# Two chunks' state products interleaved over the tile array, and a new order of the first up stage

## The chip, the cores and the metric

The kernel runs on one core of one Trainium2 chip. The metric is the device time of one execution in microseconds (us). Kernels are compared by the median of several runs.

## The reference, cut to what matters

```python
gamma = 1.0 - 2.0 ** (-5.0 - np.arange(H))            # H = 8 heads
for t in range(S):                                     # retention: q, k, v are (B=4, H=8, S=768, D=64)
    state = gamma * state + einsum('bhd,bhe->bhde', k[:, :, t], v[:, :, t])
    y[:, :, t] = einsum('bhd,bhde->bhe', q[:, :, t], state) / sqrt(D)
x = y.transpose(0, 2, 1, 3).reshape(B * S, H * D)      # 3072 tokens x 512
g = x @ w_gate                                         # 512 x 1536
out = (g * sigmoid(g) * (x @ w_val)) @ w_out           # 1536 x 512
```

The weights come as float64 words, and the kernel turns them into float32 itself.

## The kernel before

**Segments.** The tokens are worked in four segments of 768: three chunks of 128 positions of two batches each. Segment 0 has the chunks c = 0, 6, 1, 7, 2, 8 (batch 0 and batch 1 in turn; `cs[0]` to `cs[5]`). For each segment the attention makes `x`, an up stage makes the hidden values of 12 column blocks (filters f = 0 to 11), and a down stage multiplies by `w_out`. The attention of segment 1 is woven into the down stage of segment 0, and so on. The change is in segment 0, whose attention, weight conversion and up stage run together in the first 105 us or so.

**Attention of a chunk.** Transposed keys and queries lie with the two heads of a pair on partitions 0 to 63 and 64 to 127 (`half[0]`, `half[1]`); each product of a head uses the rows of its own half.
- `scores` (L633 for TensorE, PE): eight products with 64 rows into two banks, one bank per head of a pair; VectorE (DVE) multiplies each bank with the decay mask (L639). The masks are the first three pieces of the table `tab`, which is loaded in pieces A0, A1, A2, A4 (6 KB) and A3 (query decays).
- `rows_of` (L694) transposes the keys of the first two chunks on PE, so that their rows need not be loaded. `scale_k` (L654 on DVE or GpSimd, POOL; L661 on ScalarE, ACT) and `scale_q` (L648) put the decays on keys and queries.
- `state` (L715): keys times values, 64 rows of output per head. Of a batch's first chunk ACT copies it (L718), later DVE adds it (L720) to the old state that `decay` (L701, four ACT instructions) has scaled.
- `mix_old` (L730): old state times queries, eight products of 64 rows by 64 columns of the array, heads in turn, so two 64x64 tiles of the array are in use; one chunk after the other.
- `mix` (L744): values times masked scores, into the same bank; then the result is split in three parts into `xa` (ACT L1000, DVE L1007 and L401).

**Weights.** Raw halves (gate, value) of a filter are loaded (L513), and converted: ACT L534 and L537, DVE L547, ACT L540, DVE L555. Filters 0 and 1 are converted half by half, gate first. The converted block is split in three parts as a matmul operand: ACT L991, DVE L994, POOL L997.

**Up stage of segment 0.** Filters 0 and 1 go in pieces of one chunk pair (`plain_part`, L937, 12 matmuls of 256 columns each, one piece for gate and one for value); filters 2 to 11 go whole (`plain`, L919). Each piece needs all three parts of its operands, the third last.

**What sets the order.** `PLAN` is a list of steps written out by hand, and every engine's queue has its instructions in that order. `s0` is `scores(cs[0])`, `m` mix, `o` mix_old, `t` state, `r` rows_of, `g` decay, `K`, `k`, `E`, `Q`, `q` the scalings, `x` a split, `l3:1` a load of chunk `cs[3]`, `A` a table piece; `U`, `V` raw weight loads, `a`, `b`, `S`, `c`, `C` the conversion, `n` the three parts of the two halves, `p`, `v`, `u`, `y` the pieces, `G`, `W`, `i`, `j` the whole filters. Loads are issued by the sync engine (SP) in one queue (the first two query chunks by ACT), with at most eight under way: each load waits for the one eight before it. The segments after that, and the down stages, are in the same list.

**Last segment.** In its down stage, the blocks of `w_out` come by one load each (768 KB), for the first three filters by two (L1147).

Of the kernel before, what the change touches and what calls it, by code (L numbers as in the profile page):

```python
# [55 lines left out]
    C1:0 l5:2 p0:1 n1:1 u0:0 u0:1 T0:0 q5 v0:1 a2 l4:2 b2 y0:1 o5 y0:0 o4 n1:3 S2 n1:2 m5 T0:1 n1:4  # L56
    c2 m4 n1:5 x5:2 p1:0 l5:3 x5:1 p1:1 u1:0 C2 v1:0 U3:1 T0:2 x4:2 T1:0 U12:0 a3 v1:1 y1:0 x4:1
    T1:1 L b3 p0:2 a12 c12 n2:0 S3 u1:1 T1:2 b12 u0:2 U4:3 c3 Z0 n2:1 v0:2 Z1 n2:3 S12 y1:1 a4 n2:2
    p1:2 v1:2 C3 u1:2 n2:4 G2:0 y0:2 C12 G2:1 n3:0 U13:1 y1:2 n3:1 n2:5 b4 T2:0 n3:2 S4 U5:2 n3:3
    c13 T2:1 W2:0 Z12 W2:1 h0 c4 i2:1 n3:4 i2:0 G3:0 n3:5 T3:0 C4 T2:2 T3:1 U6:3 j2:0 a5 G3:1 T3:2  # L60
    j2:1 Z2 n4:0 U7:0 W3:0 i3:0 n4:1 b5 n4:2 n4:3 S5 n4:4 W3:1 i3:1 n4:5 c5 G4:0 C5 n5:0 a6 b6 a13
    l4:3 T4:0 j3:0 G4:1 n5:1 j3:1 Z3 T4:1 n5:3 i4:0 n5:2 T4:2 S6 W4:0 b13 c6 i4:1 n5:4 a7 S13 C6
    W4:1 n6:0 T5:0 U8:2 Z4 b7 U14:3 n5:5 n6:1 G5:0 j4:1 S7 C13 j4:0 G5:1 n6:2 a8 n6:3 P2 n6:4 i5:1
    c14 W5:1 i5:0 Z13 c7 j5:1 T6:0 n6:5 W5:0 a14 U9:1 U15:0 C7 T5:1 G6:0 T6:1 n7:0 T5:2 G6:1 n7:3
    n7:1 T6:2 i6:0 b8 j5:0 Z5 S8 n7:4 W6:1 b14 g4 n7:2 G7:0 i6:1 W6:0 P0 c8 S14 C8 Z6 C14 h2 a9 b9
    G7:1 j6:1 n7:5 S9 n8:0 c15 n8:3 j6:0 k5 c9 W7:1 Z14 T7:0 n8:1 C9 n8:4 U10:2 a15 n8:2 i7:1 U11:1
    W7:0 T7:1 j7:1 n8:5 i7:0 T8:0 T7:2 b15 Z7 S15 a10 n9:0 G8:0 G8:1 W8:1 i8:0 n9:3 b10 j7:0 T8:1
    n9:1 n9:2 U16:3 S10 a11 n9:4 G9:0 k4 i8:1 t4 C15 c10 C10 n9:5 W8:0 g5 n10:0 T8:2 T9:0 b11 c16
    n10:1 G9:1 Z15 j8:0 j8:1 n10:2 a16 n10:3 t5 U17:2 b16 W9:0 i9:1 T9:1 0/h0.0 T9:2 S11 Z8 W9:1 S16
    G10:1 n10:4 i9:0 C16 c11 C11 n10:5 n11:0 j9:0 Z9 G10:0 n11:3 Z16 i10:1 j9:1 a17 i10:0 W10:1 P1  # L70
    n11:4 T11:0 T11:1 1/was0.0 T11:2 n11:1 W10:0 Z11 c17 n11:2 n11:5 b17 0/h0.1 0/W0 G11:1 0/h1.0
    G11:0 j10:0 0/d0.0 h1 0/h0.2 1/sc0 j10:1 i11:0 0/h1.1 0/W1 S17 0/d1.0 i11:1 0/d0.1 1/l3 C17
    T10:0 1/dec0.0 W11:0 0/d1.1 0/d0.2 W11:1 0/h2.0 j11:0 0/D0.2 j11:1 1/k0.0 1/l4 1/dec0.1 1/q0.0
    0/D0.1 1/q0.1 0/D0.4 1/k0.1 1/l5 0/D0.0 0/h2.1 0/d1.2 0/h1.2 0/h4.0 0/W2 0/Z0 1/A0 1/y0.06
    1/new0.0 0/h4.1 1/y0.01 0/D0.5 0/D0.3 0/d2.0 1/B0 0/D1.1 0/h3.0 1/y0.03 0/D1.5 1/y0.04 0/Z1
    1/y0.02 1/y0.07 1/y0.05 T10:1 1/was0.1 1/y0.15 1/y0.00 1/y0.14 0/d2.1 0/D1.4 1/y0.12 0/d2.2
    0/D1.2 1/y0.13 0/W3 Z17 0/D1.3 0/Z2 0/d3.0 0/D1.0 0/h2.2 0/h3.1 1/C0 0/W4 T10:2 0/h3.2 0/d3.1
    0/h4.2 Z10 1/y0.16 1/l7 1/y0.17 1/new0.1 1/sum0.0 0/D2.3 0/D2.1 1/y0.10 0/h5.0 1/begin 1/sum0.1
    0/d3.2 0/h5.1 1/y0.11 0/D2.5 1/sc1 0/D2.0 0/d4.0 1/was1.0 0/D2.4 0/d4.1 0/D3.4 1/l6 1/dec1.1
    0/h5.2 1/dec1.0 0/D2.2 1/x0.2.0 0/D3.1 1/q1.1 0/d4.2 0/W5 0/D3.5 1/x0.1.0 0/h6.0 1/k1.0 0/Z3  # L80
    1/sum0.3 1/k1.1 1/sum0.2 1/x0.2.1 0/D4.5 0/D3.2 0/D3.3 0/D3.0 1/q1.0 0/Z4 0/h6.1 0/D4.0 0/D4.4
    1/x0.1.2 1/x0.1.1 1/A1 1/x0.0.0 0/d5.0 1/x0.2.2 1/y1.00 0/h6.2 1/y1.06 1/x0.0.2 1/new1.0 0/D4.2
    0/d5.1 0/d5.2 0/D4.3 0/D4.1 1/y1.07 1/y1.01 0/W6 0/h7.0 1/B1 1/x0.0.1 1/y1.04 1/y1.12 0/h7.1
    1/l9 0/d6.0 0/D5.4 0/h8.0 0/d6.1 1/y1.02 0/D5.3 0/D5.2 0/W7 0/h8.1 1/y1.05 0/d6.2 1/l8 1/l11
    0/Z5 1/y1.03 1/was1.1 0/D5.5 1/C1 0/d7.0 1/y1.16 0/d7.1 0/D6.5 0/D5.0 1/y1.17 1/y1.15 1/new1.1
    0/h7.2 1/y1.14 1/y1.11 0/D5.1 1/y1.13 1/x1.2.0 0/D6.3 0/d7.2 0/D6.4 0/Z6 1/y1.10 0/D7.3 0/h9.0
    1/sc2 0/h8.2 1/x1.2.2 0/D6.2 1/q2.1 1/k2.1 0/D7.5 0/W8 1/sum1.0 0/D6.1 1/sum1.2 1/k2.0 0/D6.0
    0/D7.1 1/x1.1.0 0/h10.0 0/h9.1 0/d8.0 0/D7.2 1/dec2.0 1/l10 1/sum1.1 1/dec2.1 0/W9 1/x1.1.1
    0/D7.0 0/d8.1 1/x1.2.1 0/Z7 1/sum1.3 1/was2.0 1/q2.0 1/x1.0.0 1/x1.1.2 0/d9.0 0/D7.4 0/d8.2
    0/h11.0 1/A2 1/new2.0 0/D8.0 1/x1.0.1 0/h10.1 0/D8.3 0/D8.2 0/d9.1 1/L0 0/D8.1 1/y2.00 0/D8.4  # L90
    1/B2 0/W10 0/d9.2 1/y2.07 1/y2.05 0/d10.0 0/D8.5 0/h9.2 1/y2.02 0/h11.1 0/D9.3 1/y2.03 0/h10.2
    1/y2.01 0/D9.5 0/Z8 1/y2.04 1/y2.06 1/w0.0.0 0/D9.4 0/d10.1 0/h11.2 1/C2 1/y2.16 1/y2.14 0/W11
# [12 lines left out]
    1/p3.4 1/u3.4 1/u2.2 1/u2.8 1/p3.5 1/u3.1 1/u3.5 1/L6 1/w5.1.0 1/p3.6 1/w4.0.2 1/u2.9 1/w4.1.2
    1/u3.6 1/w5.0.0 1/w4.2.1 1/p4.1 1/w5.0.1 1/p4.0 0/e5 2/begin 1/w5.2.0 1/w5.0.2 1/u3.8 1/p4.3
    1/u4.0 1/w5.1.1 1/u4.4 1/u3.9 1/w5.2.1 1/p4.2 1/u4.3 1/L7 1/u3.2 1/w5.1.2 1/p4.5 1/p5.0 1/u4.1
    1/p4.4 1/u4.5 1/w6.1.0 1/p5.1 1/u5.0 1/w4.2.2 1/w6.0.0 1/w6.1.1 1/p5.2 1/u5.1 1/u4.6 0/e4
    1/w6.1.2 1/u2.7 1/w6.0.1 1/w6.2.0 1/w5.2.2 1/u5.3 1/p4.6 1/p5.3 1/p5.4 1/u5.4 1/u4.8 1/p5.5
    1/u5.5 1/L8 1/w7.2.0 1/p5.6 1/u4.9 1/w6.0.2 1/u4.2 1/w7.1.0 1/w8.2.0 1/p6.1 1/u5.6 1/w7.0.0  # L110
    1/u4.7 1/w7.2.1 1/p6.0 1/u3.7 1/w7.1.1 1/w7.0.1 1/u6.0 1/w8.2.1 1/u5.2 1/u6.1 1/L10 1/p6.3
    1/w7.0.2 1/u6.4 1/u5.8 1/p6.2 1/p6.5 1/u5.9 1/u6.3 1/u6.2 1/p6.4 1/w7.2.2 1/u5.7 1/w7.1.2
    1/w8.1.0 1/w6.2.1 1/p7.0 1/u6.6 1/w6.2.2 1/p7.3 1/p7.1 1/u6.5 1/p6.6 1/u7.0 1/L9 1/w8.0.0
    1/w8.1.1 1/u7.4 1/p7.2 1/p7.5 1/w8.0.1 1/u6.8 1/w9.2.0 1/u6.9 1/u7.3 1/u7.1 1/w9.2.1 1/u7.6
    1/w8.0.2 1/p7.4 1/p8.0 1/u8.0 1/w8.1.2 1/p8.1 1/u7.5 1/w9.1.0 1/p8.3 1/w9.1.1 1/w9.0.0 1/p8.2
    1/u8.4 1/u8.3 1/p7.6 1/u7.2 1/p8.5 1/L11 1/u7.8 1/w9.1.2 1/w9.0.1 1/w8.2.2 1/p8.4 1/u8.6 1/u6.7
# [254 lines left out]
def tile_retnet_swiglu(  # L371
# [249 lines left out]
    def pairs(t):  # L621
        return t.rearrange("p (n t) -> p n t", n=NP)
# [717 lines left out]
```

## Time and profile before

| | us |
|---|---|
| median of 3 runs (lowest, highest) | 643.47 (642.88, 643.62) |
| the profiled execution | 642.54 |
| its span, first to last instruction | 640.5 |
| PE busy | 632.9 (99%) |
| DVE, ACT, POOL busy | 484.1, 394.3, 261.1 |
| first scores on PE start at | 5.78 |
| last mix of segment 0 ends, up pieces of filter 1 begin | 34.22 |
| whole filters (L919) begin | 46.14 |

PE's work is almost the whole span. In the table above, the last three rows are stages of segment 0 read from PE's timeline. In the profile's lines, `64*64` ahead of a shape is the tile of the PE array (rows by columns), a float32 matmul leaves two records (`x16` is eight matmuls), and `[0.60 <-DMA ...]` is idle time just before a row and what ended it. Times of PE's rows overlap a little, since matmuls are pipelined: the distance between two starts says more than a row's own length.

### The profile page before, as it was taken

Reading aid. Unit: us, or ns where it says so; the run is one execution under the profiler, and the core shown is the slowest. Engines: PE = TensorE matmul, PEld = TensorE weight load, DVE = VectorE, ACT = ScalarE, POOL = GpSimd, SP = SyncE. Lnnn points to the kernel's source line nnn. Section 1 sums busy time; section 2 is a strip of 40 time slices with the busy share of each in tenths; the row PEclk is TensorE's granted clock in tenths of the full one; section 3 lists DMA queues with packets and bytes.
Section 4 is the critical chain, followed back from the end, with each engine's and each line's share of the span. In section 5 each row is a group of like instructions: output and inputs, shape, how many; then the busy total and the mean of one; then the engine's idle time right before and its main releaser. Section 6 shows DMA issues by size and latency. Waiting matters only on the chain.

```text
span 640.5 us, 14132 instructions
## 1 busy us (share of the span) xinstructions
PE 632.9 (99%) x5587; PEld 580.4 (91%) x5587; DVE 484.1 (76%) x715; ACT 394.3 (62%) x868; POOL 261.1 (41%) x172
## 2 busy tenths in 40 slices
PE   7999999999999999999999999999999999999997
PEld 6899999987779999997778999998777999999886
DVE  4998787899898887665797869575789866768361
ACT  4787797777865565566766555564785555654221
POOL 1534445544425866630003665550101666663000
PEclk9999999999999999999999999999999999999999
DMA  9899998798787445258765640457776444304564
GB/s 320 291 332 326 376 329 269 268 326 305 266 285 278 168 148 173 75 179 260 247 239 214 211 152 15 175 196 246 226 258 248 154 164 173 116 1 151 194 214 148
DMA packets 50626, 139.60 MB, mean 218 GB/s; under 512 B 5120, under 2 KB 18176, under 8 KB 50560
## 3 DMA queue, kind: packets, MB, share of 16 engines
q1 hardware_dynamic: 49984, 137.92, 62.6%
q8 instruction: 44, 0.72, 0.5%
q10 hardware_dynamic: 576, 0.79, 0.3%
q14 instruction: 22, 0.18, 0.1%
HBM read 108.80 MB, written 29.88 MB: 217 GB/s over the span
## 4 chain that ended last, share of the span: by engine, by line
PE 97%; DMA 3%; SPq 0%; DVE 0%; ACT 0%; issue 0%
PE bank L1088 41%; PE bank L1157 32%; PE bank L919 13%; PE bank L789 6%; PE bank L937 3%; DMA hT<-in_v_n_dram 2%; PE bank L744 1%; DMA hT<-in_q_t_dram 1%; PE bank L730 0%; PE bank L715 0%; PE bank L633 0%; DVE chunk_x L1178 0%; SPq L513 0%; ACT chunk_x L1180 0%; SPq L466 0%
## 5 line engine op out<-in xcount | busy, mean ns | idle before, releaser
L1157 PE MATMUL bank<-oitem,gitem 128*128 128x512 f32 x867 | 208.2, 394 | 0.0
L1157 PEld LDWEIGHTS bank<-oitem,gitem 128*128 128x128 f32 x867 | 159.6, 188 | 34.5 <-DVE tmp L812 0.4
L997 POOL TENSOR_TENSOR gitem<-gitem 128x768 fp32r<-128x768 f32 x71 | 138.7, 1963 | 117.9 <-DVE gitem L994 99.0
L1088 PE MATMUL bank<-xa,gitem 128*128 128x384 f32 x864 | 160.5, 334 | 0.0
L1088 PEld LDWEIGHTS bank<-xa,gitem 128*128 128x128 f32 x864 | 150.8, 188 | 0.2
L997 POOL TENSOR_TENSOR oitem<-oitem 128x256 fp32r<-128x256 f32 (+1 forms) x60 | 64.1, 1074 | 56.8 <-DVE oitem L994 48.3
L1088 PE MATMUL bank<-xb,gitem 128*128 128x384 f32 x432 | 84.5, 334 | 0.0
L919 PE MATMUL bank<-xa,oitem 128*128 128x384 f32 x480 | 84.3, 335 | 0.0
L919 PEld LDWEIGHTS bank<-xa,oitem 128*128 128x128 f32 x480 | 83.0, 188 | 0.4 <-ACT tmp L444 0.2
L994 DVE SCALAR_TENSOR_TENSOR gitem<-gitem,loads 128x768 fp32r<-128x768 f32 x72 | 75.1, 1057 | 9.1 <-ACT gitem L991 7.5
L1088 PEld LDWEIGHTS bank<-xb,gitem 128*128 128x128 f32 x432 | 75.9, 188 | 0.4
L991 ACT ACTIVATE gitem<-loads 128x768 fp32r<-128x768 f32 x72 | 59.6, 843 | 26.0 <-PE bank L1088 16.8
L994 DVE SCALAR_TENSOR_TENSOR gitem<-gitem,hT 128x768 fp32r<-128x768 f32 x48 | 46.1, 965 | 24.4 <-ACT gitem L991 24.4
L991 ACT ACTIVATE gitem<-hT 128x768 fp32r<-128x768 f32 x48 | 40.2, 842 | 31.4 <-PE bank L1157 29.4
L1022 ACT COPY chunk_x<-bank 64x128 f32<-64x128 f32 x144 | 36.6, 260 | 32.6 <-PE bank L789 21.3
L401 DVE SCALAR_TENSOR_TENSOR gitem<-gitem 128x768 fp32r<-128x768 f32 x49 | 49.7, 1022 | 1.3 <-DVE gitem L994 0.5
L816 POOL TENSOR_TENSOR loads<-loads,tab 128x512 f32<-128x512 f32 x9 | 13.4, 1493 | 82.1 <-PE bank L789 44.6
L1088 PE MATMUL bank<-xb,oitem 128*128 128x384 f32 x216 | 43.4, 335 | 0.0
L1088 PEld LDWEIGHTS bank<-xb,oitem 128*128 128x128 f32 x216 | 37.9, 188 | 0.3
L994 DVE SCALAR_TENSOR_TENSOR oitem<-oitem,loads 128x256 fp32r<-128x256 f32 (+1 forms) x42 | 34.5, 824 | 2.1 <-ACT oitem L991 2.1
L1105 DVE TENSOR_TENSOR hT<-bank,tmp 128x384 f32<-128x384 f32 x36 | 20.0, 555 | 20.7 <-PE bank L1088 20.4
L1103 ACT COPY tmp<-bank 128x384 f32<-128x384 f32 x36 | 17.2, 478 | 28.3 <-PE bank L1088 19.3
(118 smaller groups left out, 789.8 us busy)
## 6 DMA issues: line engine op xcount, KB each, us to landing
loads<-wup SPq DMA_DIRECT2D x36, 896.0 KB, 4.7
oitem<-wdnt SPq DMA_DIRECT2D x33, 768.0 KB, 4.4
wdnt<-oitem SPq DMA_DIRECT2D x12, 768.0 KB, 5.5
wup<-first SPq DMA_DIRECT2D x9, 896.0 KB, 6.7
rawp<-in_w_gate_dram SPq DMA_DIRECT2D x12, 512.0 KB, 6.8
rawp<-in_w_val_dram SPq DMA_DIRECT2D x12, 512.0 KB, 6.2
rawp<-in_w_out_dram SPq DMA_DIRECT2D x12, 512.0 KB, 5.7
out_dram<-chunk_x SPq DMA_DIRECT2D x21, 256.0 KB, 2.1
```

What stands on the lines that cost most here:

```text
L401: stt(o, x, 1.0, y, op0=mul, op1=op)
L789: nc.tensor.matmul(o, a, b, start=start, stop=True, skip_group_check=True)
L919: nc.tensor.matmul(o, w[:, a, ts(b, P)], X0[:, a, i, NC - 1 - b], start=a == b == 0, stop=a == 2 and b == NC - 1, skip_group_check=True)
L937: nc.tensor.matmul(o, w[:, a, ts(b, P)], X0[:, a, :, NC - 1 - b, ts(j, P)], start=a == b == 0, stop=a == 2 and b == NC - 1, skip_group_che ...
L991: act(o[0], x, AF.Copy, scale=CUT / FAR)
L994: stt(o[1], f32(o[0]), -FAR, x, op0=mul, op1=add)
L997: op(o[2], f32(o[0]), f32(o[1]), op=add)
L1022: copy(cx[half[i], ds(2 * h, 2), c, half[z]], y.rearrange("p (b t) -> p b t", b=2))
L1088: nc.tensor.matmul(o, w[:, a, k], x[:, a, KH - 1 - k], start=start and a == k == 0, stop=a == 2 and k == KH - 1, skip_group_check=True)
L1103: steps = (lambda: copy(p1, x), lambda: tt(c11, z, p1, op=add), lambda: act(gate, c11, AF.Silu, scale=ONE), lambda: copy(u2, x), lambda: c ...
L1105: lambda: copy(p5, wb), lambda: tt(h1, x, p5, op=add),
L1157: nc.tensor.matmul(banks[tok][:, cols], hs[f][:, a, ds(i * TH + u * P, P)], wo[f][:, a, cols], start=f == a == 0, stop=f == NF - 1 and a = ...
```

## The change

It does four things.

1. `mix_old` takes two chunks, one of each batch, and issues their products in turn. For the second chunk each product uses the rows of the other half of the array, so that four 64x64 tiles follow each other instead of two.
2. So that the second chunk's operands lie there, the chunks 7 and 8 have their keys and queries loaded with the halves changed over (two loads of 64 rows in place of one, four times), their scores' banks are taken in changed order, the query decays and state decays are copied with the halves changed over (four ACT instructions, steps `e0`, `e1`), the states of chunks 6 and 7 are written with the halves changed over, and chunk 8's decay turns its state back (eight ACT instructions of 64 rows in place of four).
3. `PLAN` is new up to the end of the first up stage. The rest of the list is as before.
4. In the last segment the loads of `w_out` are split in two for the first seven filters instead of three.

```diff
 PLAN = """
-    A0 I0 l0:0 l1:0 A2 A1 U0:0 s0 a0:1 r1 l0:2 s1 b0:1 A4 A3 l2:1 l2:0 r0 m0 K0 S0:1 c0:1 l1:2 x0:1
-    t0 s2 E1 l3:0 l3:1 m1 l2:3 C0:1 g2 V0:0 a0:0 Q2 n0:0 b0:0 l2:2 x1:2 s3 x1:1 n0:1 l4:1 l4:0 l3:2
-    t1 S0:0 k2 x0:2 q3 c0:0 C0:0 o2 U1:1 m2 o3 n0:3 s4 m3 a1:1 n0:4 x2:1 l5:1 l3:3 b1:1 x2:2 x3:1
-    S1:1 t2 n0:2 p0:0 q4 a1:0 x3:2 c1:1 n0:5 k3 C1:1 g3 b1:0 n1:0 v0:0 l5:0 U2:3 s5 S1:0 t3 c1:0
+    l0:0 A0 l1:0 A1 I0 l0:2 A2 A4 s0 s1 U0:0 l2:0 a0:1 b0:1 m0 r0 l2:1 S0:1 l3:1 l1:2 r1 c0:1 A3
+    x0:2 l3:0 C0:1 K0 V0:0 l2:2 x0:1 l3:2 E1 s2 t0 e1 e0 m1 n0:0 t1 U1:1 Q2 a0:0 l2:3 b0:0 x1:1 l4:0
+    s3 q3 g2 l4:1 l3:3 S0:0 n0:1 c0:0 o2 n0:2 C0:0 n0:3 m2 l5:0 x1:2 m3 p0:0 a1:0 a1:1 n0:4 x2:2
+    b1:1 l5:1 x2:1 l4:2 x3:2 n0:5 k2 x3:1 S1:1 v0:0 c1:1 l5:2 C1:1 U2:3 p0:1 t2 b1:0 g3 S1:0 c1:0
+    u0:1 s4 C1:0 k3 n1:0 v0:1 q4 t3 u0:0 n1:3 y0:1 a2 s5 T0:0 n1:1 q5 T0:1 n1:2 b2 U12:0 y0:0 o4 m4
+    m5 T0:2 U3:1 p1:0 n1:4 p1:1 S2 n1:5 x5:2 Z0 x5:1 v1:0 v1:1 x4:2 c2 u1:0 x4:1 u1:1 P0 C2 y1:0 a12
 ...
-        queue.dma_start(out=t, in_=(k_t, q_t, v_n, k_n)[w][c])
+        src = (k_t, q_t, v_n, k_n)[w][c]
+        if w < 2 and turned_over(c):
+            for m in range(2):
+                queue.dma_start(out=t[half[m]], in_=src[half[1 - m]])
+            return
+        queue.dma_start(out=t, in_=src)
+
+    def turned_over(c):
+        return c // NCK % 2 == 1 and c % NCK > 0
 ...
-        "s": lambda n: scores(cs[n]), "o": lambda n: mix_old(cs[n]),
+        "s": lambda n: scores(cs[n]), "o": lambda n: mix_old(cs[n], cs[n + 1]),
-        "E": lambda n: scale_k_act(cs[n]),
+        "E": lambda n: scale_k_act(cs[n]), "e": lambda n: turn_tables(n),
 ...
+        if turned_over(c):
+            sp = sp[::-1]
 ...
-            engine.tensor_tensor(pairs(chunks[c][1]), qt, qdec, op=ALU.mult)
+            engine.tensor_tensor(pairs(chunks[c][1]), qt, qturn if turned_over(c) else qdec,
+                                 op=ALU.mult)
+
+    qturn = pairs(loads[:, :512])
+    gturn = warm[:, ds(P + 8, NP)]
+
+    def turn_tables(m):
+        act(qturn[half[m]], qdec[half[1 - m]], AF.Copy)
+        act(gturn[half[m]], gdec[half[1 - m]], AF.Copy)
 ...
+    def other(c):
+        return c // NCK % 2 == 1 and c % NCK < L - 1
+
     def decay(c):
         if 0 < c % NCK < NCK - 1:
+            new, was = state_of(c), state_of(c, 1)
             for n in range(NP):
-                nc.scalar.activation(state_of(c)[:, n], state_of(c, 1)[:, n], AF.Copy,
-                                     scale=gdec[:, ds(n, 1)])
+                if not turned_over(c):
+                    act(new[:, n], was[:, n], AF.Copy, scale=gdec[:, ds(n, 1)])
+                elif other(c):
+                    act(new[:, n], was[:, n], AF.Copy, scale=gturn[:, ds(n, 1)])
+                else:
+                    for m in range(2):
+                        act(new[half[m], n], was[half[1 - m], n], AF.Copy,
+                            scale=gturn[half[1 - m], ds(n, 1)])
 ...
-                nc.tensor.matmul(st[ds(D * i, D), n], kd[:, h], vn[:, h],
+                nc.tensor.matmul(st[half[i ^ other(c)], n], kd[:, h], vn[:, h],
                                  start=(n == 0), stop=True, skip_group_check=True)
 ...
-    def mix_old(c):
-        qd, prev = pairs(chunks[c][1]), state_of(c, 1)
-        for k, (n, i, to) in enumerate(y_parts(c)[1]):
-            r = ds(D * i, D)
-            nc.tensor.matmul(to, prev[r, n], qd[r, n], start=k < 2, stop=False,
-                             skip_group_check=True)
+    def mix_old(c, d):
+        parts = [(pairs(chunks[e][1]), state_of(e, 1), y_parts(e)[1]) for e in (c, d)]
+        for k in range(2 * NP):
+            for x, (qd, prev, to) in enumerate(parts):
+                n, i, o = to[k]
+                nc.tensor.matmul(o, prev[half[i ^ x], n], qd[half[i ^ x], n], start=k < 2,
+                                 stop=False, skip_group_check=True)
 ...
-                for i in (slice(2), slice(2, 3)) if s == NSEG - 1 and f < 3 else (slice(None),):
+                for i in (slice(2), slice(2, 3)) if s == NSEG - 1 and f < 7 else (slice(None),):
```

On PE the new order of the first steps is: scores 0 and 1, mix 0, both transposes, scores 2, state 0, mix 1, state 1, scores 3, the products of chunks `cs[2]` and `cs[3]`, mixes 2 and 3, the first up pieces; before, transposes stood between the first scores, and scores 4 ahead of the pieces. On DVE three operations (L547, L1007, L555) now stand between the first masks and the scaling of the first keys (L654). In SP's queue the first keys are ahead of the table, the first values and the 6 KB of A4 are ahead of the first raw weights, and the load of the first keys of segment 1 moves up to the early part of the stage.

More of the change, by code (lines that the diff above doesn't have):

```diff
@@ L57 @@
[L57 to L92, printed above, removed]
@@ L631, in scores @@
             for i in range(2):
-                r = ds(D * i, D)
+                r = half[i]
                 nc.tensor.matmul(sp[i][:, ts(n, P)], kt[r, n], qt[r, n],
@@ L756, in tile_retnet_swiglu @@
     spare = tab[:, : 2 * 512]
-    half = [ds(0, D), ds(D, D)]
     given = {}
```

310 lines of the change are left out of this document (172 added, 138 removed).

## The prediction

> **What bounds the kernel now.** I read the page first, then the chain that ended last, then TensorE's, VectorE's and ScalarE's timelines of the first 46 us, then a table by stretches. The page gives PE 632.9 us of a span of 640.5 us, 99%. So time can be won only by giving PE less to do, or in the 7.6 us in which it stands still. The chain says where those are:
>
> ```profile
> 0.73 3.83 DMA hT<-in_q_t_dram
> 4.58 5.10 DMA hT<-in_v_n_dram
> 10.54 7.39 DMA hT<-in_v_n_dram
> 22.66 3.06 PE bank L937 x24
> ...
> 34.29 11.85 PE bank L937 x96
> 46.14 58.37 PE bank L919 x336
> ```
>
> Columns: start, length, what. Transfers are on the chain only before 18 us; from 22 us on it is matmul behind matmul. PE's timeline of the start:
>
> ```profile
> 1.08 3.78 PE L1253 MATMUL bank<-warm 128*128 128x128 f32 x16 [1.08 <-DVE warm L1268]
> 5.78 1.16 PE L633 MATMUL bank<-hT 64*128 64x128 f32 x16 [0.92 <-DMA hT<-in_k_t_dram]
> 9.81 1.09 PE L744 MATMUL bank<-tmp,hT 128*64 128x128 f32 x16 [0.60 <-DMA hT<-in_v_n_dram]
> 11.93 1.16 PE L633 MATMUL bank<-hT 64*128 64x128 f32 x16 [0.50 <-DMA hT<-in_k_t_dram]
> 14.47 1.16 PE L633 MATMUL bank<-hT 64*128 64x128 f32 x16 [0.36 <-DVE tmp L639]
> 17.97 1.09 PE L744 MATMUL bank<-tmp,hT 128*64 128x128 f32 x16 [0.63 <-DMA hT<-in_v_n_dram]
> 30.43 1.96 PE L730 MATMUL bank<-loads,states 64*64 64x128 f32 x32
> 32.32 1.09 PE L744 MATMUL bank<-loads,chunk_x 128*64 128x128 f32 x16
> 34.22 10.97 PE L937 MATMUL bank<-xa,oitem 128*128 128x256 f32 x88
> ```
>
> The bracket is the idle time before a row and what ended it; one matmul leaves two records. First scores at 5.78, then 0.60 + 0.50 + 0.36 + 0.63 = 2.1 us of waits, then none. At 34.22 all attention of segment 0 and four pieces of the up stage (L937) are behind PE. The changed order has done exactly the same work when its last L744 ends, so I compare the two there.
>
> **1. The old states' products (L730).** 32 matmuls in all. The pair at 30.43 takes 32.32 - 30.43 = 1.89 us for 32 records, 59 ns each, two array tiles at work (rows and columns of one head together). After: four different 64x64 tiles follow each other. Nearest row, also four 64x64 tiles in turn but with 64 columns:
>
> ```profile
> 175.92 1.52 PE bank L789 x80
> ```
>
> That is 19 ns a record. At twice the columns, 38 ns, 32 records take 1.2 us; with two tiles' time just halved, 0.95 us. I take 1.05: 0.85 us less for the pair at 30.43, and as much for the first two (1.09 us at 16.25, and 20.02 - 18.99 = 1.03). PE's work shrinks by about 1.8 us (1.4 to 2.0; none if the tiles don't overlap).
>
> The Trainium skill (TensorE: Matmul & The Clock Gate, Part 3) says that a weight load overlaps running matmuls only when its row group differs. By that rule, two of each four tiles share rows and would queue, L730 would keep its 1.9 us a pair, and the forecast would lose 1.8 us of PE work. L789's 19 ns, with tiles that share rows as well, speaks against it.
>
> **2. What is added.** Four ACT copies that turn two tables: two of 64x512 and two tiny ones. Nearest rows:
>
> ```profile
> L769 ACT COPY local<-tab x2: 620/622/625, 51.9 to 126.3; 64x512 f32<-64x512 f32 x2
> L772 ACT ACTIVATE local<-tab x1: 191/191/191, 87.7 to 87.7; 128x4 f32<-128x4 f32 x1
> ```
>
> 2 x 0.62 + 2 x 0.19, less some 0.08 overlap each: 1.4 us of ACT. They lie between a state's copy and ACT's next work and hold up what follows (step 4). The decay of chunk 8's state is 8 ACT instructions instead of 4, at 1.05 us per four (L701): +1.05 us late in the stage, where ACT is busy 47.26 of 58.86 us; hidden. Four loads become two halves of 64 rows each: four more issues on SP at 0.33 to 0.43 us. Split loads of this sort (L786) exist; a pair of halves in a full queue lands in 0.7 to 1.0 us where a whole one takes 0.68. I charge 0.05 us each; SP's queue holds more than 3 us of data throughout, so issue is covered. In the last segment four more weight loads are split, four more issues; from 589.40 to 637 PE shows no gap there: nothing. The first load for segment 1 (512 KB, 1.4 us of queue time) moves from 82 us to about 36, ahead of the fifth filter's raw halves; those wait for ScalarE to free their buffer until 37.2 in any case.
>
> **3. When data arrive in the new order.** SP's queue is full (DMA share 0.93 up to 16 us) and is served in order, so an arrival is the sum of what is ahead. The first two transfers land at 4.4 to 4.56 us; after that, in the trace's landing marks, 256 KB take 0.68 us, 128 KB 0.34, the 6 KB table 0.23, and 512 KB of raw weights 1.5 to 1.66. In the order of the change: k0 4.56 (before 5.65, A0 stood ahead of it), A0 and q1 5.9, k1 6.64, v0 7.65 (before 9.67), A2 8.0, and the gate weights, before at 8.98, get v0 and the 6 KB ahead of them: 8.98 + 0.67 + 0.23 = 9.85. Then q2 at 11.2, v1 12.6, A3 13.1, k3 13.9, the other raw half 15.4. At 16 to 18 us one landing lagged by 1.1 us in this trace (the 7.39 above against 5.4 median); I leave that lag in, so v2 is at 17.2.
>
> **4. PE's new chain to the first up pieces.** Scores 0 run when the warm-up is done, at 4.7 instead of 5.78: 1.1 us won. Scores 1 wait for k1 (6.7 to 7.8). Mix 0 needs its second mask product (L639), which needs A2: DVE 8.05 to 8.7, mix 8.75 to 9.7. Transposes to 10.85, scores 2 with q2 from 11.2 to 12.25. Now state 0 (L715) needs the scaled keys, and VectorE's queue has changed ahead of them. Before, they came straight after the masks:
>
> ```profile
> 9.99 0.69 DVE L654 TENSOR_TENSOR hT<-bank,tab 128x512 f32<-128x512 f32 x1
> 10.67 0.69 DVE L547 SCALAR_TENSOR_TENSOR bank<-first,bank 128x512 uint32<-128x512 uint32 x1
> ```
>
> After, three operations are queued ahead, two of them on the gate weights: ACT L534 at 9.87 and L537 to 11.03; DVE L547 11.05 to 11.75; ACT L540 to 12.45; DVE L555 12.5 to 13.2; only then the keys, 13.1 to 13.8. State 0 starts at 13.85: a new wait of 1.6 us. ACT then copies state 0 (to 14.9), does the four turns (to 16.25), L1000 and L991 (to 17.35), state 6's copy (to 17.65); POOL's turned q is ready at 17.5 to 17.9. The four-tile products, begun at 17.1, go on from there: wait 0.7, done at 18.8; mixes to 20.65. First up piece 20.65 to 22.2. The next needs its third weight part: DVE L994 to 22.4, POOL L997 (1.3 us) to 23.7: wait 0.5, done 24.25. From there: L937 1.55, L715 0.6, L633 1.1, L937 1.55, L715 0.6, L633 1.1, products 1.05, two mixes 1.9 = 9.45 us, with each input there in time (the tightest VectorE's last split of chunk 3, 24.75 for 24.76): **33.7**. Against 34.22 that is 0.5 us won; waits after the start rise from 2.1 to about 5 us and eat most of the 1.1 of the start and the 1.8 of step 1. The next piece waits some 0.1 us more for n1's third part (DVE 33.4, POOL 34.7), while the switches between 64x64 and 128x64 tiles become two fewer at about 0.1 us each (32.11 + 0.11 to 32.32). Net **0.6 us** won.
>
> **5. The rest of the stage.** From 34.22 to 105 PE has no idle time to win, so it can only lose:
>
> ```profile
> 34.22:46.14 11.92, 11.92 (x99) 11.83 (x98) 10.67 (x18) 10.82 (x15) 4.55 (x3) 1.00 0.95 335
> 46.14:105.00 58.86, 58.86 (x352) 58.43 (x351) 48.03 (x68) 47.26 (x71) 28.50 (x20) 1.00 0.96 339
> ```
>
> Columns: length, busy PE, PEld, DVE, ACT, POOL, clock, DMA share, GB/s. DVE is free 10.8 us of 58.9 here, which is the cover. Carried on by rows, DVE begins the third filter's L547 at 34.8 (before 32.23), yet the third filter's last weight part is made by POOL at about 44.5 (before 44.2), with PE there at 45.5 and needing it 1.4 us later. Lead 1 to 2.4 us. I charge nothing.
>
> **Sum.** The profiled execution took 642.54 us (span 640.5 and 2.0 around it); 642.54 - 0.6 = 641.9. The three timed runs have a median of 643.47, 0.93 above it; on that footing the forecast is **642.9 us**.
>
> **Rivals.**
> A, the forecast: 0.2 to 1.25 us won, chance 0.42.
>
> B, the queue ahead of the keys is shorter than I make it. ScalarE's first weight row shows how much hangs on that arrival:
>
> ```profile
> 9.00 0.67 ACT L534 ACTIVATE first<-rawp 128x512 f32<-128x512 f32 x1 [5.84 <-DMA rawp<-in_w_gate_dram]
> ```
>
> If the gate weights land 1 us sooner than 9.85, state 0 waits 0.6 instead of 1.6 and all that hangs on it up to 23.7 moves too; with the waits for state 6 and POOL halved, 0.6 + 1.0 + 0.6 = 2.2 won: 641.3. For: arrivals are my least certain terms. Against: the bytes ahead of these weights only grew. Chance 0.30.
>
> C, slower: VectorE falls behind in the third to fifth filter. Place: the third weight part at L919's first row. Price: past the lead of 2.4 us PE waits one for one; if VectorE is 5 us later than before there, 2.6 lost less 0.6 won: 645.5. It decides from 3 us on. For: it idles 1 us more before 34 us, and its L547 comes 2.6 us later. Against: 18% free time after. Chance 0.15.
>
> D, the change doesn't do what it says, the four tiles queue up (also by the page's rule in step 1): 1.8 us of work comes back, of which the 0.5 us wait for POOL and 0.1 of the next hide 0.6: 642.9 + 1.2 = 644.1. L789 speaks against. Chance 0.08.
>
> E, the clock. Sixteen records of 128 columns take 3.78 us in the warm-up and 1.16 in the scores, where two run at a time: 0.21 us between starts against 0.11 between pairs. So PE begins at half rate, for some 3.6 us. If a stand-still brought that back once, 3.6 us at half rate would lose 1.8: 644.7. No row shows such a fall, PEclk stands at 9 throughout, and the longest new wait, 1.6 us, has work on both sides. Chance 0.05. The Trainium skill (TensorE: Matmul & The Clock Gate, Part 1) puts the fall after an idle window of about 3.4 us; by that rule it doesn't come.
>
> This kernel's measurement can tell about 0.2%, 1.3 us, from no change. Faster by more: B, 0.30. Slower by more: C, 0.15. Within: A, D and E, 0.55. The range goes from 641.0 (B) to 645.0 and leaves out the far half of C and a little beyond B.
>
> **What would show it.** L730 as x64 records at 27 to 38 ns each; PE's first scores near 4.7; a wait before the first L715 of 1 to 2 us that VectorE ends, and one before the first L730 that ACT or POOL ends; the end of the last L744 at 33.2 to 34.2; no PE gap after. I am wrong if state 0 starts before 12.8 (then B), if L715 waits for something else, or if PE waits at L919.

## The result, and the profile after

The changed kernel takes 644.09 us (median of 22 executions, 642.84 to 648.15) against 642.81 of the kernel before beside it (22 executions, 641.38 to 644.97). The ratio is 1.0023, interval 1.0013 to 1.0034: **slower by 0.2%**, 1.3 us, where the forecast had 0.6 us won. The time itself lies in the range of 641.0 to 645.0; the direction is wrong.

The profiled execution took 643.23 us (before 642.54), with a span of 641.4. PE's timeline of the changed kernel (start, length, then engine, line, operation and tile, and in brackets the idle time before the row and what ended it):

```profile
4.80 3.16 PE L643 MATMUL bank<-hT 64*128 64x128 f32 x32
12.04 1.16 PE L643 MATMUL bank<-hT 64*128 64x128 f32 x16 [1.05 <-DMA hT<-in_q_t_dram]
14.04 0.69 PE L745 MATMUL bank<-hT 128*64 128x64 f32 x16 [0.84 <-DVE hT L674]
18.16 1.10 PE L761 MATMUL bank<-loads,states 64*64 64x128 f32 x30 [0.65 <-ACT states L748]
24.34 2.24 PE L967 MATMUL bank<-xa,oitem 128*128 128x256 f32 x16 [0.40 <-POOL oitem L1027]
31.54 1.10 PE L761 MATMUL bank<-loads,states 64*64 64x128 f32 x32
32.58 1.09 PE L775 MATMUL bank<-tmp,chunk_x 128*64 128x128 f32 x16
34.47 1.72 PE L967 MATMUL bank<-xa,oitem 128*128 128x256 f32 x10
```

Two things are as drawn up. The scores begin at 4.80 instead of 5.78, and the second pair of products takes 32.58 - 31.54 = 1.04 us instead of 1.89: four tiles overlap. But four waits stand between, and the mark (the end of segment 0's last mix, where the same work is done in both) is at 34.47 instead of 34.22. So 0.98 + 2 x 0.85 us were won (the first pair taken like the second) and more than that lost in the same 30 us. After the mark PE falls behind a little more, 0.37 us at 128 and 0.56 at 588, and the span ends 4.05 us after the start of the last matmul instead of 3.75.

The rows of VectorE and ScalarE that answer to those shown of before, each from its engine's timeline, and the decay of chunk 8's state from the answer on its line (lowest, median and highest ns, first and last start):

```profile
13.30 0.68 DVE L674 TENSOR_TENSOR hT<-bank,tab 128x512 f32<-128x512 f32 x1
```

```profile
9.91 0.68 ACT L544 ACTIVATE first<-rawp 128x512 f32<-128x512 f32 x1 [6.75 <-DMA rawp<-in_w_gate_dram]
```

```profile
L731 ACT ACTIVATE states<-states,warm x8: 345/346/350, 81.1 to 83.6; 64x64 f32<-64x64 f32 x8
```

The keys of chunk 0 are scaled at 13.30 (before 9.99), behind the weight's conversion; the first gate weights are there at 9.91 (before 9.00).

The profile is one execution, and it shows 0.69 us of the 1.28. The rest is in the other executions. The records of TensorE's clock give each a mean granted clock. Eleven of the 22 have 0.9985 or more, with a median of 643.50 us; the other eleven have 0.996 or 0.997, with a median of 645.06. One stretch of 3.4 us at half rate in 641 gives 1 - 0.5 x 3.4 / 641 = 0.997. The kernel before has no such execution among the 125 beside the experiments.

### The profile page after: what moved, and what is told of

Same layout as the page of the kernel before. It is cut to its first block, busy times and chain, and to the rows that moved or that the text cites. A ratio compares the mean times of both kernels' runs of the same rounds, so it can differ in the third digit from the quotient of the medians.

```text
span 641.4 us, 14167 instructions
## 1 busy us (share of the span) xinstructions
PE 632.9 (99%) x5587; PEld 580.2 (90%) x5587; DVE 486.7 (76%) x715; ACT 397.0 (62%) x876; POOL 260.6 (41%) x172
## 4 chain that ended last, share of the span: by engine, by line
PE 96%; ACT 1%; DMA 1%; DVE 1%; issue 0%; POOL 0%; SPq 0%
PE bank L1118 41%; PE bank L1187 32%; PE bank L949 13%; PE bank L819 6%; PE bank L967 2%; DMA rawp<-in_w_gate_dram 1%; DMA hT<-in_q_t_dram 1%; PE bank L745 0%; PE bank L643 0%; PE bank L775 0%; POOL oitem L1027 0%; ACT first L550 0%; ACT first L544 0%; ACT oitem L1021 0%; ACT loads L667 0%
## 5 line engine op out<-in xcount | busy, mean ns | idle before, releaser
L1027 POOL TENSOR_TENSOR oitem<-oitem 128x256 fp32r<-128x256 f32 (+1 forms) x60 | 65.5, 1099 | 59.4 <-DVE oitem L1024 50.2
```

The lines of the kernel that those rows point to most:

```text
L1027: op(o[2], f32(o[0]), f32(o[1]), op=add)
```

## The experiments

They were timed in five groups (e1 to e4, e5 to e8, e9 to e11, e12, e13 to e15), each beside the kernel before on the group's own chip. The ratio on record is not the quotient of the two medians: the two differ by up to 0.0006 (e5, e7, e11). "Mark" is the start of the up pieces behind the last mix of segment 0, in the one profiled execution. It varies with the first loads: by the traces' landing marks the first gate weights land between 9.2 and 10.8 us in the profiles of the new order, and e8 and e15, the same kernel, have 33.61 and 33.91. "Half clock" counts executions with a mean granted clock under 0.9985.

| kernel | us | before | ratio (interval) | mark | half clock |
|---|---|---|---|---|---|
| e1 order alone | 644.29 | 643.00 | 1.0023 (1.0012 to 1.0033) | 35.25 | 5 of 12 |
| e2 products alone | 649.03 | 643.00 | 1.0091 (1.0076 to 1.0107) | 39.25 | 6 of 6 |
| e3 changed, whole loads | 644.15 | 643.00 | 1.0019 (1.0010 to 1.0027) | 35.10 | 4 of 11 |
| e4 products, whole loads | 647.71 | 643.00 | 1.0070 (1.0055 to 1.0085) | 39.04 | 5 of 6 |
| e5 keys first | 643.24 | 642.87 | 1.0000 (0.9989 to 1.0012) | 34.12 | 0 of 12 |
| e6 the same, whole loads | 642.94 | 642.87 | 1.0001 (0.9989 to 1.0014) | 33.74 | 0 of 12 |
| e7 changed, waits filled | 643.38 | 642.87 | 1.0002 (0.9988 to 1.0015) | 33.78 | 0 of 12 |
| e8 order, keys first | 642.07 | 642.87 | 0.9985 (0.9972 to 0.9998) | 33.61 | 0 of 12 |
| e9 = e8 with split tail | 642.89 | 643.01 | 1.0001 (0.9992 to 1.0010) | 33.45 | 0 of 11 |
| e10 = e8 with turns | 643.92 | 643.01 | 1.0015 (1.0006 to 1.0024) | 35.71 | 0 of 11 |
| e11 second pair only | 642.67 | 643.01 | 1.0001 (0.9989 to 1.0013) | 34.02 | 0 of 12 |
| e12 the same, decays on DVE | 645.24 | 643.22 | 1.0035 (1.0021 to 1.0048) | 34.60 | 0 of 5 |
| e13 both pairs, no turns | 641.63 | 642.78 | 0.9986 (0.9976 to 0.9996) | 33.53 | 0 of 12 |
| e14 both pairs, turns on POOL | 642.25 | 642.78 | 0.9993 (0.9984 to 1.0002) | 32.78 | 0 of 12 |
| e15 = e8 again | 642.33 | 642.78 | 0.9995 (0.9985 to 1.0005) | 33.91 | 0 of 12 |

**The two halves of the change (e1 to e4).** e1 is the kernel before with the new order, products not interleaved, loads whole:

```diff
-PLAN of before
+PLAN of after, with "o2 o3" for o2, "o4 o5" for o4, without e0, e1
```

> The new order of the first up stage with the old products: one chunk after the other, whole loads, no turned tables. The mark is the start of the up pieces after the last mix of segment 0: 34.22 us before, 34.47 after. Theory H (the split loads of 64 rows slow the load queue and cost the changed kernel about 0.8 us; the order itself is sound): the mark comes at 34.9, that is 34.47 less 0.8 for the split loads, and 1.2 more for the products that no longer overlap. Theory Q (the new order itself costs the time, the split loads nothing): 35.7, and the time is about 0.3% above before.

The order alone gives a loss as large as that of the full change: 1.0023. Two waits stand out on PE:

```profile
12.30 1.16 PE L455 MATMUL bank<-hT 64*128 64x128 f32 x16 [1.46 <-DMA hT<-in_q_t_dram]
14.92 0.69 PE L537 MATMUL bank<-hT 128*64 128x64 f32 x16 [1.46 <-DVE hT L476]
```

Scores 2 wait for queries 2 and state 0 for the keys. The mark is between the two theories' figures, but both waits hang on loads that came late in this execution (gate weights at 10.79, in the changed kernel's profile at 9.88), so it decides nothing between them.

e2 is the other half, the kernel after with before's order and three split filters:

```diff
-... o2 U1:1 m2 o3 ... g2 V0:0 ... o5 y0:0 o4 ...
+... U1:1 o2 m2 ... e0 e1 g2 V0:0 ... y0:0 o4 ...
```

> The order of before with only the products of two chunks interleaved and what they need: split loads, turned tables, turned states. H: 1.7 us of TensorE's work gone, some 0.8 of it eaten by the split loads: mark at 33.3. Q: mark at 32.5, since order is what cost the time. If the products do not overlap: 34.2 or later.

Both theories failed, by 6 us. The turns of the tables, put into ScalarE's queue, hold up the copy of state 1, which interleaved products need at once:

```profile
21.02 1.98 PE L583 MATMUL bank<-loads,states 64*64 64x128 f32 x30 [3.07 <-ACT states L570]
```

The row holds a second thing: 30 records in 1.98 us, where the same products take 1.10 elsewhere. The clock's records have half rate from 20.39 to 27.21 us. In the 3.41 us before that PE was busy for 0.98. So e2 says little of the products as such, but it shows a fall of the clock that the prediction had put at 0.05.

e3 is the changed kernel, and e4 is e2, with the chunks 7 and 8 laid out turned in DRAM, so that no load is halved:

```diff
-        if w < 2 and turned_over(c):
-            for m in range(2):
-                queue.dma_start(out=t[half[m]], in_=src[half[1 - m]])
-            return
```

> The changed kernel, with the keys and queries of chunks 7 and 8 laid out with changed halves in the input, so that each is one whole load again. H: scores 2 start at 11.3 instead of 12.04, mark at 33.7, time 0.8 us below the changed kernel. Q: mark at 34.4, time as the changed kernel's.

> The order of before, interleaved products, whole loads. Both H and Q: mark at 32.5, 1.7 us ahead of before, and the time 1.7 us (0.26%) below before. If TensorE only waits elsewhere for what it saves: mark at 33.5 to 34.2.

The halved loads do hold up the queue. From the landing of the gate weights to that of keys 3 it takes 5.4 to 6.1 us in the three profiles of this order with halves (5.79 in the changed kernel's), and 4.0 to 4.3 in the eleven with whole loads (4.04 in e3). Scores 2 run 0.7 us earlier in e3 (11.35), but state 0 starts at 14.06 as in the changed kernel, since the keys are scaled at 13.33: the wait only changed its place. The time stayed, as theory Q had it, and e4 is 6.5 us behind the mark of both theories. In e3's profiled execution the clock falls too. The stretches (length, busy PE, PEld, DVE, ACT, POOL, granted clock, DMA share, GB/s):

```profile
11.05:14.46 3.41, 1.56 (x28) 1.40 (x30) 3.03 (x5) 3.01 (x11) 0.00 (x0) 1.00 1.07 377
```

```profile
14.40:17.90 3.50, 3.50 (x48) 3.38 (x46) 2.61 (x5) 2.92 (x8) 1.14 (x1) 0.51 1.07 365
```

In the 3.41 us before the fall PE is busy for 1.56, and its longest single stand-still is 1.55 us. For the next 3.41 us (14.46 to 17.88 in the clock's records) it is granted half the rate: mix 1 takes 1.93 us for 16 records instead of 1.09. e4 stands for the state's copy for 3.14 us and has the clock fall as e2. What a fall costs is not the same everywhere: in e3 the four executions with one have a median of 644.30 us and the seven without 644.14, in e1 644.97 and 643.83, in the changed kernel 645.06 and 643.50. Why it is so little in e3 is open.

**The clock and the keys (e5 to e8).** e7 puts eight idle products into three of the changed kernel's stand-stills and moves nothing:

```diff
-... r1 c0:1 ... s2 t0 e1 ... o2 ...
+... r1 w w w c0:1 ... s2 w w t0 e1 ... w3 w3 w3 o2 ...
+    w: mm(banks[n or 6][:, :P], warm[:, :P], warm[:, :P], True)
```

> The changed kernel with eight idle products (zeros times zeros, into a bank that is free there) put into three stand-stills of TensorE: 3 before the scores of chunk 2, 2 before state 0, 3 before the first old states' products; some 0.2 us each, less than each stand-still, so nothing waits for them. Theory G: the clock does not fall any more, all executions have a mean granted clock over 0.9985, and the median is that of the changed kernel's undisturbed executions, 643.5 (0.5 above before), instead of 644.1. Theory W alone: no change, 644.1, or slower by up to 0.4 where the idle products outlast a wait.

No execution of twelve falls any more, and the median is 643.38, against 643.50 of the changed kernel's own undisturbed executions. Two stretches of the same kind, the changed kernel's and e7's:

```profile
10.60:14.05 3.45, 1.56 (x22) 1.16 (x20) 2.65 (x5) 3.18 (x11) 0.00 (x0) 1.00 1.06 266
```

```profile
10.40:13.80 3.40, 3.10 (x43) 2.67 (x43) 3.07 (x5) 2.97 (x11) 0.00 (x0) 1.00 1.05 281
```

The first is about the emptiest stretch of this length in the changed kernel's profile, and yet this execution kept the clock. The reason can be read from the clock's records: in every profile of this case the stretches between changes of the rate are multiples of 3.413 us (10.24, 6.83 and 3.41 in e3 and e2), so the rate changes in steps counted from the first grant of the full rate. In this execution that is at 6.85 us, and the emptiest step has 1.89 us busy, not 1.56:

```profile
10.26:13.68 3.42, 1.89 (x23) 1.49 (x21) 2.27 (x4) 3.14 (x10) 0.00 (x0) 1.00 1.08 281
```

Counted in such steps up to 30 us in all 17 profiles, those with 0.98 (e2), 1.17 (e4) and 1.56 us busy (e3) were followed by half rate, and those with 1.89 (here), 1.95 and 1.96 (e1) or more were not. Where the steps lie differs from one execution to the next, which fits a fall in eleven of 22; the other executions have no profile that could show it. With 3.10 busy nothing falls. Work that computes nothing makes the kernel faster by some 0.7 us in the median (the two kernels before stand at 642.81 and 642.87), though the two intervals overlap a little.

e5 takes away the wait itself. Two steps move together: the keys go ahead of the conversion on VectorE, and state 0 into the stand-still before scores 2; e6 does it with whole loads, e8 in the order alone:

```diff
-... m0 r0 l2:1 S0:1 l3:1 l1:2 r1 c0:1 A3 x0:2 l3:0 C0:1 K0 V0:0 ... E1 s2 t0 e1 ...
+... m0 r0 K0 l2:1 S0:1 l3:1 l1:2 r1 c0:1 t0 A3 x0:2 l3:0 C0:1 V0:0 ... E1 s2 e1 ...
```

> The changed kernel with one step moved: the keys of chunk 0 are scaled on VectorE ahead of the first weight's conversion instead of behind it, and state 0's products stand ahead of the scores of chunk 2 on TensorE, where 1.05 us was stood for queries 2. Theory W (the loss is this queue and nothing else): keys at about 10.5 to 11.2, state 0 at about 11.3 inside the old stand-still, the stand-still of 0.84 before it gone; the mark (x96 group) between 33.6 (all of 0.84 won) and 34.2 (if keys 3, landed at 15.67, hold scores 3), the time 642.2 to 642.9. Theory H (the halved loads hold the chain whatever VectorE does): the stand-still moves to scores 3, mark 34.3 to 34.5, the time within 0.2 of the changed kernel. Theory G (half of the changed kernel's executions fall to half clock for one window, which costs 1.6 us each): the new order leaves fewer and shorter stand-stills between 10 and 15 us, so few executions with a mean granted clock under 0.9985, and the median falls by about 0.8 more than the profile's mark shows.

> The same with the turned chunks laid out on the host, so that every load is whole (128 rows). If H holds in part, scores 2 at about 11.4 (queries 2 land 0.5 to 0.7 earlier) and keys 3 land 1.2 earlier, so that scores 3 start near 14.9 instead of 16.0: mark about 33.2, time 641.8. If the loads' shape does not matter: as the kernel with split loads, within 0.2 us.

> The kernel of the order alone (before's products and whole loads in the new order; 644.3, mark 35.25) with the same move of chunk 0's keys and state 0. Theory W: the stand-still of 1.46 before state 0 goes, and of the 1.46 before scores 2 some 0.6 is filled by state 0; mark 33.9 to 34.4, time 642.4 to 643.0, so the order's whole loss is where the keys stand on VectorE. If something else of the order costs the time (the queue's new order, the later third chunk of work), mark over 34.8 and time over 643.6.

In e5 state 0 runs inside the old stand-still, and what waits now is mix 1, for values 1:

```profile
11.23 0.69 PE L567 MATMUL bank<-hT 128*64 128x64 f32 x16 [0.34 <-DVE hT L496]
12.02 1.16 PE L465 MATMUL bank<-hT 64*128 64x128 f32 x16
13.91 1.09 PE L597 MATMUL bank<-tmp,hT 128*64 128x128 f32 x16 [0.73 <-DMA hT<-in_v_n_dram]
```

The clock falls no more, and the time is that of the kernel before (ratio 1.0000). So two theories hold at once: the queue on VectorE made the wait, and the wait made the clock fall. W's mark came (33.6 to 34.2), its time of 642.2 to 642.9 did not. Of H, whole loads bring mix 1 forward to 12.60 in e6, but the medians differ by 0.30 us, less than either interval is wide. e8 is the surprise: without the products, the same order is faster than before (642.07), and so 0.87 us faster than e6, which has 1.7 us less matmul time.

**Where the products' gain goes (e9 to e15).** e9 adds only the split loads of the last segment to e8 (`f < 3` becomes `f < 7`), e10 only the four ScalarE turns, whose output nobody reads:

> The order with chunk 0's keys first (642.07, before's own products) with the w_out loads of the last segment split for seven filters instead of three, nothing else. Between that run and the one with the products interleaved as well (642.94) 0.87 us are unexplained, of which the mark shows only 0.13. Theory T: the splits cost 0.3 to 0.5 us at the end of the program (the last store lies that much further behind the last product): 642.4 to 642.6. Theory A (ScalarE's turns carry all of it): no change, 642.1 within 0.2.

> The order with chunk 0's keys first (mark 33.61, 642.07) plus the four ScalarE instructions that turn the tables, at the place where the changed kernel has them; nobody reads what they write, the products stay as before. Theory A: their 1.4 us delay the copy of state 1 and the second weight's conversion behind it on ScalarE, the first old states' products of the second chunk stand about 0.5, and the up pieces wait for their third part: mark 34.2 to 34.7, time 642.7 to 643.1, so the turning eats what interleaving gives. Theory T (the turns hide, as the prediction had it up to a wait of 0.7): mark within 0.3 of 33.61, time 642.1 to 642.4.

In e9's profile the span ends 4.04 us after the start of the last matmul, in e8's 3.75: 0.28 us. All six profiles with seven split filters have 4.03 to 4.05 there. Of the eleven with three, nine have 3.75 to 3.81, but e12 has 3.95 and e2 4.05. So some 0.28 us go with the split loads in every profile but e2's, and what makes them is not shown. Against before, e9's median stands 0.68 us worse than e8's (-0.12 against -0.80), of which 0.28 is seen there; the other 0.4 is within the intervals.

e10's turns cost far more than they last. First e8, then e10, ScalarE's timeline; then PE's of e8 and of e10:

```profile
15.41 0.43 ACT L540 COPY states<-bank 128x256 f32<-128x256 f32 x1
```

```profile
15.54 0.63 ACT L474 ACTIVATE loads<-tab 64x512 f32<-64x512 f32 x1
18.04 0.35 ACT L545 COPY states<-bank 128x256 f32<-128x256 f32 x1
```

```profile
20.13 4.72 PE L759 MATMUL bank<-xa,oitem 128*128 128x256 f32 x36
```

```profile
24.72 2.23 PE L764 MATMUL bank<-xa,oitem 128*128 128x256 f32 x16 [0.41 <-POOL oitem L824]
```

The copy of state 1 is 2.6 us later, 1.7 to 1.9 without the late start of that execution (0.74 us at mix 0, 0.93 at ScalarE's first weight row). The second weight's conversion follows the copy on ScalarE, so the up pieces, one unbroken row in e8, wait for POOL's third part. The mark is 2.1 us later, 1.2 to 1.4 without the late start. That is most of the 1.7 us that interleaving gives. The times say the same: from 0.80 us under before (e8) to 0.91 above it, with intervals that do not touch.

e11 tried to keep the gain: e8 with only the second pair interleaved, only chunk 8 turned (whole loads), the turns at 19 and 23 us.

```diff
-        return c // NCK % 2 == 1 and c % NCK > 0
+        return c // NCK % 2 == 1 and c % NCK == 2
-        return c // NCK % 2 == 1 and c % NCK < L - 1
+        return c // NCK % 2 == 1 and c % NCK == 1
```

> A version meant to beat both: the order with chunk 0's keys first, the first pair of old states' products separate as before, only the second pair interleaved over four tiles; only chunk 8 has its rows turned (whole loads, turned in the layout), the tables are turned on ScalarE at two places where it stands still at 19 and 23 us, state 7's decay turns (8 instructions instead of 4), the tail splits stay at three filters. Theory A: everything up to 24.8 as in 642.07's run, then 0.85 us less for the second pair: mark 32.8, time 641.0 to 641.4. If the eight decay instructions or the later turns delay the conversion: mark over 33.2 and time over 641.6.

> The version with only the second pair interleaved, with one thing mended: the decays that carry a state to the other half of the partitions (states 7 and 8) are two VectorE instructions of 64x256 each in place of eight of 64x64 on ScalarE, which took 2.89 us there and ended in a wait of 0.84 before the second pair. Theory A (ScalarE's queue is what the interleaving pays with): ScalarE's next conversion step goes from 29.2 back to some 26.3, the second pair starts at 29.8 without a wait and takes 1.05; mark 32.7 to 32.9, time 641.1 to 641.5, faster than both kernels. If VectorE, now with some 0.8 us more, is late instead: mark 33.2 to 33.6, time 641.7 to 642.3.

Both missed. The state must then change halves between chunks 6 and 7, and eight instructions of 64x64 take 2.89 us on ScalarE (four of 128x64 take 1.05). The conversion behind them is late, the addition to state 7 stands behind that on VectorE, and the second pair waits. In e12 two instructions of 64x256 on VectorE take 1.79 us for state 7 and 3.16 for state 8, and VectorE is late at 85 us, with a gap of 0.92 us on PE; the other profiles from e5 on have none over 0.22 between 36 and 130 us. ScalarE's timeline of e11 and PE's, then VectorE's of e12 and PE's:

```profile
26.31 2.89 ACT L548 ACTIVATE states<-states,tab 64x64 f32<-64x64 f32 x8
```

```profile
30.77 1.43 PE L578 MATMUL bank<-loads,states 64*64 64x128 f32 x32 [0.84 <-DVE first L383]
```

```profile
80.05 3.16 DVE L549 TENSOR_TENSOR states<-states,warm 64x256 f32<-64x256 f32 x2
```

```profile
85.00 23.18 PE L768 MATMUL bank<-xa,oitem 128*128 128x384 f32 x132 [0.92 <-DVE hT L266]
```

The last three ask whether the interleaving itself is at fault. e13 is e6 with three split filters and without the turns (chunks 7 and 8 get their neighbours' decay, so part of the computation is changed); e14 makes the turns on POOL:

```diff
-        act(qturn[half[m]], qdec[half[1 - m]], AF.Copy)
-        act(gturn[half[m]], gdec[half[1 - m]], AF.Copy)
+        nc.gpsimd.tensor_copy(qturn[half[m]], qdec[half[1 - m]])
+        nc.gpsimd.tensor_copy(gturn[half[m]], gdec[half[1 - m]])
```

> Both pairs interleaved in the order with chunk 0's keys first, whole loads, tail splits for three filters, and the four table turns left out: chunks 7 and 8 are scaled by the tables as they are, so part of the computation is changed (these heads get their neighbours' decay) while every other instruction stays. Theory A (the turns on ScalarE take the gain): state 1's copy back at 15.4, products 16.3 to 17.4, no wait before them; against the order alone (mark 33.61) 0.85 for each pair, less at most 0.6 of waiting for the third part of the first up pieces, made by POOL at 20.4 and 22.6 as there: mark 31.9 to 32.6, 1.0 to 1.7 us less than e15. Rival I (the interleaving itself or the conversion eats it): mark 33.2 or later, less than 0.5 under e15.

> The same with the turns made, but on POOL, which stands still until 13.4 and from 14.7 to 19.1: two copies of 64x512 and two tiny ones ahead of the scaling of chunk 7's queries (between 0.6 and 1.3 us each, by POOL's 1.27 for a product of 128x512). ScalarE's queue is that of the order alone. Theory A: the scaled queries of chunk 7 are ready 1.3 to 2.7 us later than without turns, at 16.0 to 17.4, products done at 17.4 to 18.5 (order alone 18.23), the second pair 0.85 shorter: mark 32.6 to 33.2, 0.4 to 1.0 us less than e15, faster than both kernels of this case. Rival I: as e15 or later.

> The order with chunk 0's keys first, products as before, once more on the chip of these two: 642.1, about 0.8 under before, mark 33.4 to 33.8.

e14's POOL, then its PE:

```profile
13.60 0.60 POOL L485 COPY loads<-tab 64x512 f32<-64x512 f32 x1 [13.15 <-DMA tab<-in_decays_dram]
```

```profile
17.02 1.10 PE L579 MATMUL bank<-loads,states 64*64 64x128 f32 x30 [0.21 <-POOL loads L478]
32.78 12.04 PE L785 MATMUL bank<-xa,oitem 128*128 128x256 f32 x96
```

A turn takes 0.60 us on POOL as on ScalarE, but it stands in a queue that is empty. State 1's copy is back at 15.45, the first pair waits 0.21 us, and the mark is 1.13 us ahead of e15's, some 0.3 of it by earlier loads (gate weights at 9.94 and 10.22). e13's mark is 0.4 ahead in an execution whose gate weights came 0.75 later than e14's (ScalarE's first row at 10.71 instead of 9.96). The profiled executions are no fair sample: e14's is the fastest of its twelve (641.23), e13's the slowest (643.22). In the medians e13 is 0.70 under e15, short of theory A's 1.0 to 1.7, and e14 is 0.08 under it where A had 0.4 to 1.0; the intervals overlap. So the place of the turns is shown in the traces, but whether e14 is faster than e15 is not settled by the times.

Is a version faster than both kernels? e8 is, in its own comparison, but its repeat, e15, is 0.45 us under before with an interval that takes in 1. e14, with the full change apart from the two queues, the whole loads and the tail, is 0.53 under before, its interval up to 1.0002. All three are under the changed kernel's ratio of 1.0023, with intervals that do not touch its own.

## Why the prediction was wrong, step by step

**Step 1, the products: right.** 0.85 us less a pair was forecast; 1.04 against 1.89 was measured. Rival D, in which the tiles queue up, falls with it. The rule of the Trainium skill (TensorE: Matmul & The Clock Gate, Part 3), read as step 1 read it, would have kept the 1.89; the measurement decides.

**Step 2, what is added: wrong in three places.** The halves of a load were charged 0.05 us each. Two halved loads lie between the gate weights and keys 3, and they cost 1.4 to 2.0 us there, 0.7 to 1.0 each. With whole loads scores 2 run 0.7 us earlier (e3) and mix 1 some 1.3 earlier (e6 against e5, some 0.3 of it by the start), though little of that reaches the end. The Trainium skill (DMA: Bandwidth & Descriptors, Rules for kernel authors) advises one transfer of 128 partitions over two of disjoint halves; these rows agree. The last segment's splits were put at nothing, and some 0.28 us go with them at the end of the program. The eight ScalarE pieces were put at 1.05 us more than the four; they take 2.86 us, 1.8 more, and no gap of PE shows it at 81 us.

**Step 3, arrivals: right up to 10 us, short after.** Gate weights at 9.85 forecast (the sum as written gives 9.88), landed at 9.88. Then queries 2 at 11.2 forecast, landed at 11.90; values 1 at 12.6, landed at 13.48; keys 3 at 13.9, landed at 15.67. In e3, with whole loads, the same three land at 11.21, 12.58 and 13.95: the arrivals were right but for the halves of step 2.

**Step 4, the chain to 33.7: the step that failed.** Its queues were drawn rightly: keys at 13.30 (forecast 13.1), state 0 at 14.04 (13.85), state 1's copy at 17.66 (17.35), a POOL wait of 0.40 (0.5). The waits behind the scores come to 3.5 us (0.55, 1.05, 0.84, 0.65, 0.40), no more than the 4.1 forecast there. What failed is the sum: from the keys to the mixes the links were 0.2 to 0.45 late, the three up pieces with the wait among them took 5.42 us instead of 5.15, and the mark came 0.77 late, so that a gain of 0.5 became a loss of 0.25. A chain without slack was added up from rounded rows with 0.5 us to spare. The wait for the keys that this step named was taken as given. In the order alone the two steps that remove it are worth 2.1 us in the medians against before (+1.29 in e1, its falls of the clock included, -0.80 in e8); it need not be there, because VectorE stood idle for 1.25 us ahead of the conversion. The turns, too, were taken as delays to be borne: e10 shows that they cost 1.2 to 1.4 us of the mark, and e14 that an engine with an empty queue can take them.

**Rival E, at 0.05 and left out of the sum, was half of the result.** Its price was right: 1.8 us forecast for one fall, 1.56 between the medians of the two groups of executions. Its chance was not. The prediction took "PEclk stands at 9 throughout" as evidence about waits that the kernel before does not have, and counted the longest single wait (1.6 us). e3 and e7 show that a step of 3.4 us with less than half of it busy (1.56) is enough. The Trainium skill (TensorE: Matmul & The Clock Gate, Part 1) has the free-running window of 3413 ns, and the half rate comes in just such lengths (3.41 in e3, 6.83 in e2). But it puts the fall after an idle window, and here PE worked 1.56 us of the window; the measurement decides.

**Step 5 and rivals B and C.** C did not come: from the mark to 128 us 0.12 us were lost. B's condition, gate weights a whole us sooner, did not come either.

Added up in medians against before: changed +1.28; without the fall +0.5 (e7); without the wait as well +0.37 (e5); whole loads +0.07 (e6); turns off ScalarE and the tail back, -0.53 (e14). By the ratios it is +1.5, +0.1, 0.0, +0.1 and -0.45. Steps of 0.3 in this sum are inside the intervals; the first, the fall of the clock, is also counted execution by execution.

## What to carry to other kernels

Work taken from the engine that is the bound is worth only what its preparation does not put into another engine's full queue: follow each new instruction to the one queued behind it, and look for an engine that stands still at that time. When a change adds stand-stills to TensorE, add up its busy time over every 3.4 us, not only the longest gap; under about half of it (here 1.56 us fell, 1.89 did not), expect half rate for a stretch in some executions, and look at the granted clock of all of them, since one profile can miss it.

## What was not expected of the hardware

- The clock's records show full rate first granted between 4.0 us (e15) and 10.2 us (e2) in different executions, though the matmuls begin at 1.1 us in all of them. At half rate, 3.41 us with PE busy for 2.51 (e4) or 2.78 us (e2) were followed by another 3.41 at half rate; those followed by full rate have 2.89 (e15) or more in all 17 profiles.
- Moving a state to the other half of the partitions in 64x64 pieces takes 346 ns each on ScalarE, eight in 2.86 us; pieces of 128x64 that stay in place take 336 ns each, but overlap more (four in 1.05 us) and do twice the work.
- On POOL a copy of 64x512 takes 0.60 us, the same as ScalarE's 0.63.
